# Attention and a fast three-way product on TensorE: where weights, tokens and split q and k begin in SBUF

## The chip, the core and the metric

The kernel runs on one core of one Trainium2 chip. The metric is the device time in microseconds (us) of one launch, as the median of several runs. The profile is of one execution on the same core; its span reaches from the first to the last instruction.

## What is computed

Sigmoid attention over 8 sequences, 12 heads, 448 positions, 64 values a head, and then a layer with three weight matrices and a maximum over them:

```python
scores = scale * np.matmul(q, k.transpose(0, 1, 3, 2)) - np.log(S)
attn = 1.0 / (1.0 + np.exp(-scores))
attn_out = np.matmul(attn, v).astype(np.float32)
...
x = np.ascontiguousarray(attn_out.transpose(0, 2, 1, 3)).reshape(B * S, H * D)
h = np.maximum(np.maximum(x @ w1, x @ w2), x @ w3)
return (h @ w_out).astype(np.float32)
```

There are 3584 tokens of 768 values, the four matrices are 768 x 768, and everything is float32.

## The kernel before

The program has two halves, and TensorE works in both without a pause.

**Attention** (24 steps of four heads, the loop over `fours`). Two tiles `qk` are loaded a step, each with two heads on the 128 partitions (64 partitions a head) and q and k side by side, 448 columns each. For float32 accuracy out of the faster float32r matmuls, `qk_split` (lines 287 to 297) cuts a tile into `hi` (a CAST to float32r, line 293) and `lo` (the rest, a subtraction, line 294); both are 896 columns long, q first, k behind it. `scores` (line 312) then computes k times q as three matmuls into one bank: hi with hi, lo with hi, hi with lo. The stationary operand (the weights that are loaded into the array) is a slice of 128 columns of k, the moving operand all 448 columns of q; each comes as a pair, one for the head in the lower 64 partitions and one for that in the upper 64. The last 64 rows of k go as plain float32 (`last_scores`, line 325). ACT takes the sigmoid out of PSUM (line 282), and `weigh` and `last_weigh` (lines 336 and 347) multiply it with v, as plain float32 matmuls of 64 x 64 in groups of four. DVE and ACT also decode and split the first weights meanwhile. The first step of attention splits its tiles in parts (`parts`), all other 46 tiles are split whole.

**Products** (four stages of four pairs of sequences, 16 visits, three outputs `q` a visit). Each visit uses a scheme with seven products of blocks (`PRODUCTS`) instead of eight. A product (lines 466 to 479) is nine matmuls at line 476 with three blocks of 128 rows: `wlo` with `xhi`, `whi` with `xlo`, `whi` with `xhi` for each. The stationary operand is a slice of 128 columns of a split weight tile (`whi`, `wlo`: 384 columns), the moving operand a slice of 448 columns of a split token tile (`xhi`, `xlo`: 3 x 448 columns). So there are 16 * 3 * 7 * 9 = 3024 matmuls, each with other weights than the one before. Twice in the program (`wide`) the first matmul of a product takes 478 columns instead of 448; the extra 30 columns of PSUM are not read.

**Where tiles stand.** Pools are laid out in SBUF in the order in which they are opened (lines 69 to 73): all split weights (`w`), the weight stage (`ws`), tokens (`xs`), results (`m`), and then split tokens (`xo`). The pools of attention come behind; when they are closed, the second halves of `xs` and `xo` and the small tiles of the products are laid over them. In bytes per partition, a split weight tile is 1536 long, a stage tile 1536, a token tile 5376, a result tile 1792, `qk`, `hi` and `lo` 3584.

Of the kernel before, what the change touches and what calls it, by code (L numbers as in the profile page):

```python
# [8 lines left out]
F32 = mybir.dt.float32  # L9
F32R = mybir.dt.float32r  # L10
# [3 lines left out]
ALU = mybir.AluOpType  # L14
# [3 lines left out]
P = 128  # L18
D = 64

LEAST = 1.125 * 2.0**-15

PRODUCTS = (
    ("a11", "b11", 0),
# [10 lines left out]
def attention_then_maxout(  # L35
# [9 lines left out]
    nc = tc.nc  # L45
    B, NK = qk.shape[0], qk.shape[1]
    S = qk.shape[3] // 2
# [6 lines left out]
    pin = tc.keep_in_program_order  # L54
# [11 lines left out]
    def pool(stack, name, bufs, **kw):  # L66
        return stack.enter_context(tc.tile_pool(name=name, bufs=bufs, **kw))
# [2 lines left out]
    ws_p = pool(ctx, "ws", 1)  # L70
    xs_p = [pool(ctx, "xs", 1)]
    m_p = pool(ctx, "m", 1)
    xo_p = [pool(ctx, "xo", 1)]
    ps_av = pool(ctx, "ps_av", 1, space=PSUM)

# [47 lines left out]
    def decoding(dec_p, todo, bufs, ahead, square_p):  # L123
# [11 lines left out]
        def decode(raw, out):  # L135
# [17 lines left out]
            pin(nc.vector.scalar_tensor_tensor(  # L153
                out=out, in0=square, scalar=LEAST**2, in1=bits.bitcast(F32),
                op0=ALU.is_ge, op1=ALU.mult,
# [79 lines left out]
    def attention(stack):  # L235

        qk_p = pool(stack, "qk", 4)
        hl_p = pool(stack, "hl", 2)
# [41 lines left out]
        def sigmoid(banks, **kw):  # L280
            a = a_p.tile([P, 2, S], F32, name="last" if kw else "a", **kw)
            pin(nc.scalar.activation(  # L282
                out=a, in_=banks[:, :, :S], func=AF.Sigmoid, bias=bias_s, scale=scale
            ))
            return a

        def qk_split(t, parts=(slice(0, 2 * S),)):

            hi = hl_p.tile([P, 2 * S], F32R, name="hi")
            lo = hl_p.tile([P, 2 * S], F32R, name="lo")  # L290
            for cols in parts:
                high = hi[:, cols]
                pin(nc.vector.tensor_copy(out=high, in_=t[:, cols]))
                pin(nc.vector.tensor_tensor(
                    out=lo[:, cols], in0=t[:, cols], in1=high.bitcast(F32), op=ALU.subtract
                ))
            return (hi, hi), (hi, lo), (lo, hi)

        def accumulators():
            return ps_av.tile([P, 2, 512], F32, name="ps_av")  # L300
# [1 line left out]
        def halves(ps):  # L302
            return [ps[:, e] for e in range(2)]

        def scores(terms, c, banks=None):
            if banks is None:
                banks = ps_s.tile([P, 2, 512], F32, name="ps_s")
            bank = halves(banks)
            for n, (kt, qt) in enumerate(terms):
                for e in range(2):  # L310
                    r = slice(e * D, (e + 1) * D)
                    pin(nc.tensor.matmul(  # L312
                        bank[e][:, :S], kt[r, S + c * P : S + (c + 1) * P], qt[r, :S],
                        start=n == 0, stop=n == len(terms) - 1,
                    ))
            return sigmoid(banks)
# [36 lines left out]
        loads = {}  # L353
# [26 lines left out]
        for n in range(12):  # L380
            e = n % 2
            idle = nc.const_aps.tensor(0.0, [D, P], F32, start_partition=e * D)
            pin(nc.tensor.matmul(ps[:, e, :P], idle, idle, start=True, stop=True))  # L383
        xs, lasts = {}, {}
        terms = [[(loads[0][0],) * 2]]
        end = len(fours) - 1
        for n in range(len(fours)):
            ts = loads.pop(n)
# [12 lines left out]
            if n == 0:  # L401
                chunks = [slice(S + c * P, S + (c + 1) * P) for c in range(1, C)]
                split = qk_split(ts[0], [slice(0, S)] + chunks)
                terms = (terms[0],) + (split,) * (C - 1)
                cut = S + P
                terms += (qk_split(ts[1], (slice(0, cut), slice(cut, S + C * P))),)
            else:
                terms = (terms[0],) * C + (terms[1],)
            first = [scores(terms[c], c) for c in range(C)]
            if n == 0:  # L410
                held = accumulators()
                last_scores(ts, held)
                load(n + 2)
                vts[n + 1] = load_v(*fours[n + 1])
            ahead = loads.get(n + 1)
            after = [qk_split(ahead[0]) if ahead else None]
            second = []
            for c in range(C):
                second.append(
                    scores(terms[C], c, accumulators() if n and c == 0 else None)  # L420
                )
                if n == c == 0:
                    lasts[n] = sigmoid(held, bufs=2)
            after.append(qk_split(ahead[1]) if ahead else None)
            terms = after
# [30 lines left out]
    with ExitStack() as stack:  # L456
        xs, finish = attention(stack)
# [202 lines left out]
```

## Time and profile before

| | us |
|---|---|
| median of 3 runs | 864.51 (864.01 to 864.61) |
| span of the profiled execution | 861.9 |
| TensorE busy in it | 857.6 |
| DVE busy | 619.9 |
| ACT busy | 413.3 |
| POOL busy | 173.5 |

The profiled execution has no other time of its own than its span; the median of the runs is 2.6 us above it, for what lies before the first and behind the last instruction. Busy shares overlap, as the engines work at the same time. A matmul is shown from its start to the (modelled) end of its results, and the next one starts before that end, so the distance of starts tells the rate, not the length.

### The profile page before, as it was taken

How to read it: one execution, taken by the hardware profiler on the slowest of the kernel's cores; microseconds unless marked ns; L12 is line 12 of the kernel's file. 1: busy time of each engine (PE TensorE's matmuls, PEld its weight loads, DVE VectorE, ACT ScalarE, POOL GpSimd, SP SyncE). 2: the span in 40 equal slices, each digit the busy share in tenths (PEclk: the TensorE clock that was granted, in tenths of full speed). 3: DMA queues.
4: the chain of work that ended last, by engine and by line, in shares of the span. 5: the costliest groups of instructions: out<-in, count | busy, mean ns of one | idle time of the engine just before them, and what ended most of it. 6: DMA issues, size and time to landing. Idle time of an engine off the chain costs nothing.

```text
span 861.9 us, 14260 instructions
## 1 busy us (share of the span) xinstructions
PE 857.6 (99%) x5446; PEld 706.5 (82%) x5446; DVE 619.9 (72%) x885; ACT 413.3 (48%) x545; POOL 173.5 (20%) x148
## 2 busy tenths in 40 slices
PE   9999999999999999999999999999999999999998
PEld 5555555555579999999999999999999999999997
DVE  5677668877795775787887698778778887736542
ACT  6888888888862340423434252234325252423310
POOL 0010020202115337121000021200002544560600
PEclk9999999999999999999999999999999999999999
DMA  8657776786684537326563823465472516153412
GB/s 293 209 209 242 246 253 231 257 295 220 214 288 175 184 147 250 125 75 205 207 248 113 324 80 97 161 254 198 161 290 99 186 43 238 69 202 123 154 65 86
DMA packets 74628, 161.96 MB, mean 188 GB/s; under 512 B 6976, under 2 KB 54080, under 8 KB 74560
## 3 DMA queue, kind: packets, MB, share of 16 engines
q1 hardware_dynamic: 74416, 160.94, 53.0%
q8 instruction: 43, 0.70, 0.3%
q14 instruction: 25, 0.20, 0.1%
q10 hardware_dynamic: 144, 0.11, 0.0%
HBM read 109.90 MB, written 51.12 MB: 187 GB/s over the span
## 4 chain that ended last, share of the span: by engine, by line
PE 99%; DVE 0%; DVEq 0%; issue 0%
PE ps_y L476 71%; PE ps_s L312 9%; PE ps_s L336 7%; PE ps_av L336 6%; PE ps_s L347 2%; PE ps_s L325 2%; PE ps_av L312 2%; PE ps_s L383 0%; PE ps_av L325 0%; PE ps_av L347 0%; DVE m L548 0%; DVEq L656 0%
## 5 line engine op out<-in xcount | busy, mean ns | idle before, releaser
L476 PE MATMUL ps_y<-xhi_t,whi_s 128*128 128x448 f32 x432 | 157.9, 365 | 0.0
L476 PE MATMUL ps_y<-xhi_t,wlo_s 128*128 128x448 f32 (+1 forms) x432 | 157.8, 365 | 0.0
L476 PE MATMUL ps_y<-xlo_t,whi_s 128*128 128x448 f32 x432 | 157.8, 365 | 0.0
L282 ACT ACTIVATE a<-ps_s,bias_s 128x896 f32<-128x896 f32 x121 | 114.5, 1016 | 10.2 <-PE ps_s L312 10.2
L476 PE MATMUL ps_y<-xhi_b,wlo_a 128*128 128x448 f32 x288 | 105.3, 366 | 0.0
L476 PE MATMUL ps_y<-xlo_b,whi_a 128*128 128x448 f32 x288 | 105.2, 365 | 0.0
L476 PE MATMUL ps_y<-xhi_b,whi_a 128*128 128x448 f32 x288 | 105.2, 365 | 0.0
L583 ACT COPY p<-ps_y 128x448 f32<-128x448 f32 x48 | 25.5, 531 | 157.6 <-PE ps_y L476 157.6
L108 POOL TENSOR_TENSOR ws_s<-ws_a,ws_a 128x384 f32<-128x384 f32 x12 | 14.2, 1180 | 417.9 <-DMA ws_a<-w_dram 312.8
L476 PEld LDWEIGHTS ps_y<-xhi_t,whi_s 128*128 128x128 f32 x432 | 81.2, 188 | 6.4
L476 PEld LDWEIGHTS ps_y<-xlo_t,whi_s 128*128 128x128 f32 x432 | 81.2, 188 | 6.4
L476 PEld LDWEIGHTS ps_y<-xhi_t,wlo_s 128*128 128x128 f32 x432 | 81.2, 188 | 6.3
L557 DVE TENSOR_TENSOR m<-ps_y,u 128x448 f32<-128x448 f32 x71 | 43.9, 621 | 53.3 <-PE ps_y L476 53.3
L544 ACT COPY m<-ps_y 128x448 f32<-128x448 f32 x24 | 12.8, 533 | 124.8 <-PE ps_y L476 112.6
L586 DVE TENSOR_TENSOR u<-ps_y,p 128x448 f32<-128x448 f32 x48 | 29.9, 623 | 53.9 <-PE ps_y L476 50.3
L196 POOL TENSOR_TENSOR xs_t<-xs_b,xs_t 128x448 f32<-128x448 f32 x48 | 59.8, 1272 | 38.9 <-PE ps_s L325 26.8
L231 DVE TENSOR_TENSOR xlo_t<-xs_t,xhi_t 128x1344 fp32r<-128x1344 f32 x42 | 66.7, 1589 | 0.0
L231 DVE TENSOR_TENSOR xlo_b<-xs_b,xhi_b 128x1344 fp32r<-128x1344 f32 x42 | 66.5, 1584 | 0.0
L142 ACT ACTIVATE c<-wraw 128x384 f32<-128x384 f32 x48 | 27.4, 570 | 75.5 <-DVE m L563 44.0
L336 PE MATMUL ps_av<-a,v 64*64 64x448 f32 x576 | 62.6, 536 | 0.0
L227 ACT CAST xhi_t<-xs_t 128x1344 fp32r<-128x1344 f32 x41 | 54.2, 1323 | 12.4 <-PE ps_y L476 8.8
L336 PE MATMUL ps_s<-a,v 64*64 64x448 f32 x576 | 59.7, 545 | 0.0
(89 smaller groups left out, 1769.0 us busy)
## 6 DMA issues: line engine op xcount, KB each, us to landing
qk<-qk SPq DMA_DIRECT2D x47, 448.0 KB, 4.6
xs_b<-x_dram SPq DMA_DIRECT2D x30, 672.0 KB, 6.9
wraw<-w SPq DMA_DIRECT2D x36, 384.0 KB, 4.8
xs_t<-t_dram SPq DMA_DIRECT2D x18, 672.0 KB, 8.0
v<-v SPq DMA_DIRECT2D x24, 448.0 KB, 5.5
h_dram<-m SPq DMA_DIRECT2D x48, 224.0 KB, 1.9
xs_b<-h_dram SPq DMA_DIRECT2D x16, 672.0 KB, 6.2
x_dram<-m SPq DMA_DIRECT2D x47, 224.0 KB, 3.0
```

Source lines behind the costliest of these rows:

```text
L142: pin(nc.scalar.activation(out=square, in_=high.bitcast(F32), func=AF.Square))
L196: pin(nc.gpsimd.tensor_tensor(out=r[name][:, k], in0=r[in0][:, k], in1=r[in1][:, k], op=ALU.subtract))
L227: pin(copy(out=hi, in_=r[name]))
L231: pin(nc.vector.tensor_tensor(out=lo, in0=x, in1=hi.bitcast(F32), op=ALU.subtract))
L282: pin(nc.scalar.activation(out=a, in_=banks[:, :, :S], func=AF.Sigmoid, bias=bias_s, scale=scale))
L312: pin(nc.tensor.matmul(bank[e][:, :S], kt[r, S + c * P : S + (c + 1) * P], qt[r, :S], start=n == 0, stop=n == len(terms) - 1,))
L325: pin(nc.tensor.matmul(ps[g * D : (g + 1) * D, e, :S], t[r, S + C * P :], t[r, :S], start=True, stop=True,))
L336: pin(nc.tensor.matmul(ps[e * D : (e + 1) * D, :S], vt[rows, (g * C + c) * 2 + e], chunks[c][rows, e], start=c == 0 and not (ahead and r = ...
L476: pin(nc.tensor.matmul(ps[:, :cols], wt[:, k * P : (k + 1) * P], moving, start=first and n == 0, stop=n == len(terms) - 1, skip_group_chec ...
L557: pin(nc.vector.tensor_tensor(out=m[name], in0=y, in1=add, op=ALU.add))
L583: pin(nc.scalar.copy(out=p1, in_=ps[0][:, :S]))
L586: pin(nc.vector.tensor_tensor(out=u2, in0=ps[1][:, :S], in1=p1, op=ALU.add))
```

## The change

An unused tile of 16 words (64 bytes) is opened between the results and the split tokens. All tiles behind it move by 64 bytes, the split tokens among them; weights stay. In attention, `hi` and `lo` become 1024 columns long, and where a tile is split whole, k begins at column 496 (`KEYS`) instead of 448, so 48 words between q and k are not used. Both split instructions then write two pieces of 448 columns, with a gap, instead of one of 896. `scores` gets q and k as two views. Where a tile is split in parts (the first step), k stays at column 448. The plain float32 matmuls read `qk`, `a`, `last` and `v`, which only move as a whole.

```diff
+SHIFT = 16
+
+KEYS = 496
...
     m_p = pool(ctx, "m", 1)
+
+    pool(ctx, "shift", 1).tile([P, SHIFT], F32, name="shift")
     xo_p = [pool(ctx, "xo", 1)]
...
-        def qk_split(t, parts=(slice(0, 2 * S),)):
-
-            hi = hl_p.tile([P, 2 * S], F32R, name="hi")
-            lo = hl_p.tile([P, 2 * S], F32R, name="lo")
-            for cols in parts:
-                high = hi[:, cols]
-                pin(nc.vector.tensor_copy(out=high, in_=t[:, cols]))
+        def qk_split(t, parts=None):
+
+            hi, lo = [hl_p.tile([P, 1024], F32R, name=name) for name in ("hi", "lo")]
+            if parts is None:
+                at, src = KEYS, t[:].rearrange("p (e c) -> p e c", e=2)
+                out = [x[:, : 2 * KEYS].rearrange("p (e c) -> p e c", e=2)[:, :, :S] for x in (hi, lo)]
+                views = [(src, *out)]
+            else:
+                at, views = S, [[x[:, cols] for x in (t, hi, lo)] for cols in parts]
+            for src, high, low in views:
+                pin(nc.vector.tensor_copy(out=high, in_=src))
                 pin(nc.vector.tensor_tensor(
-                    out=lo[:, cols], in0=t[:, cols], in1=high.bitcast(F32), op=ALU.subtract
+                    out=low, in0=src, in1=high.bitcast(F32), op=ALU.subtract
                 ))
-            return (hi, hi), (hi, lo), (lo, hi)
+            (hk, hq), (lk, lq) = [(x[:, at : at + S], x[:, :S]) for x in (hi, lo)]
+            return (hk, hq), (hk, lq), (lk, hq)
...
-                        bank[e][:, :S], kt[r, S + c * P : S + (c + 1) * P], qt[r, :S],
+                        bank[e][:, :S], kt[r, c * P : (c + 1) * P], qt[r],
...
-        terms = [[(loads[0][0],) * 2]]
+        terms = [[(loads[0][0][:, S:], loads[0][0][:, :S])]]
```

No instruction is added, removed or moved on any engine. The one thing that reads otherwise in the order of the instructions is the shape of the 46 whole splits on DVE, here of the second step of attention:

```order
18 L293 CAST hi<-qk 128x896
19 L294 TENSOR_TENSOR lo<-qk,hi 128x896
20 L293 CAST hi<-qk 128x896
21 L294 TENSOR_TENSOR lo<-qk,hi 128x896
22 L144 TENSOR_SCALAR wb<-wraw 128x384
```

and the same place with the change:

```order
18 L304 CAST hi<-qk 128x2x448
19 L305 TENSOR_TENSOR lo<-qk,hi 128x2x448
20 L304 CAST hi<-qk 128x2x448
21 L305 TENSOR_TENSOR lo<-qk,hi 128x2x448
22 L151 TENSOR_SCALAR wb<-wraw 128x384
```

The rows stand at the same places; only the shapes of the four splits differ.

## Rows read from the trace of the kernel before

**Rows 1.** The page: busy time, granted clock in 40 slices, chain that ended last.

```profile
PE 857.6 (99%) x5446; PEld 706.5 (82%) x5446; DVE 619.9 (72%) x885; ACT 413.3 (48%) x545; POOL 173.5 (20%) x148
...
PEclk9999999999999999999999999999999999999999
...
PE 99%; DVE 0%; DVEq 0%; issue 0%
PE ps_y L476 71%; PE ps_s L312 9%; PE ps_s L336 7%; PE ps_av L336 6%; PE ps_s L347 2%; PE ps_s L325 2%; PE ps_av L312 2%; PE ps_s L383 0%; PE ps_av L325 0%; PE ps_av L347 0%; DVE m L548 0%; DVEq L656 0%
```

**Rows 2.** Windows of 100 us in the products, all engines: work and instructions of each.

```profile
core 0: us, PE busy (x) PEld busy (x) DVE busy (x) ACT busy (x) POOL busy (x), PEclk, DMA share, GB/s
250.00:350.00 100.00, 100.00 (x495) 92.76 (x494) 66.87 (x82) 26.46 (x30) 49.85 (x40) 1.00 0.55 201
...
550.00:650.00 100.00, 100.00 (x495) 92.75 (x494) 74.79 (x111) 33.90 (x46) 6.32 (x7) 1.00 0.64 231
650.00:750.00 100.00, 100.00 (x496) 92.72 (x495) 82.99 (x104) 43.87 (x58) 45.64 (x34) 1.00 0.35 122
750.00:850.00 100.00, 100.00 (x495) 92.74 (x494) 47.98 (x55) 26.63 (x30) 26.78 (x24) 1.00 0.36 129
```

**Rows 3.** Timeline of TensorE: the first product and the beginning of the second.

```profile
start us, us, engine line op out<-in xcount [idle before <-releaser]
...
245.18 0.48 PE L476 MATMUL ps_y<-xhi_b,wlo_a 128*128 128x448 f32 x1
245.49 0.36 PE L476 MATMUL ps_y<-xlo_b,whi_a 128*128 128x448 f32 x1
...
247.14 0.38 PE L476 MATMUL ps_y<-xhi_t,wlo_s 128*128 128x478 f32 x1
247.36 0.36 PE L476 MATMUL ps_y<-xlo_t,whi_s 128*128 128x448 f32 x1
```

**Rows 4.** Timeline of TensorE: 32 starts near 300 us (first, last), and the program's last matmul.

```profile
299.64 0.37 PE L476 MATMUL ps_y<-xlo_t,whi_s 128*128 128x448 f32 x1
...
305.92 0.36 PE L476 MATMUL ps_y<-xhi_t,whi_a 128*128 128x448 f32 x1
...
858.00 0.37 PE L476 MATMUL ps_y<-xhi_b,whi_s 128*128 128x448 f32 x1
```

**Rows 5.** Timeline of TensorE in attention: 17 pairs of line 312 (first, last).

```profile
66.11 0.36 PE L312 MATMUL ps_s<-lo,hi 64*128 64x448 f32 x2
...
69.35 0.36 PE L312 MATMUL ps_s<-hi,lo 64*128 64x448 f32 x2
```

**Rows 6.** Timeline of TensorE in attention: plain float32 matmuls, merged where they repeat.

```profile
60.81 1.31 PE L336 MATMUL ps_s<-a,v 64*64 64x448 f32 x12
61.94 0.54 PE L347 MATMUL ps_s<-last,v 64*64 64x448 f32 x2
```

**Rows 7.** Lines 476 and 312: duration ns min/median/max, first and last start.

```profile
L476 PE MATMUL ps_y<-xlo_t,whi_s x432: 360/365/370, 247.4 to 852.3; 128*128 128x448 f32 x144
...
L476 PE MATMUL ps_y<-xhi_t,whi_s x432: 361/365/370, 247.6 to 852.5; 128*128 128x448 f32 x144
...
L312 PE MATMUL ps_s<-lo,hi x240: 354/362/468, 5.2 to 239.3; 64*128 64x448 f32 x120
...
L312 PE MATMUL ps_s<-hi,lo x240: 356/362/367, 5.4 to 239.5; 64*128 64x448 f32 x120
```

**Rows 8.** Groups by form: the splits on DVE, and weight loads that waited for one.

```profile
line engine op names shapes xcount | busy us, mean ns | idle before us <-releasers
...
L294 DVE TENSOR_TENSOR lo<-qk,hi 128x896 fp32r<-128x896 f32 x46 | 51.1, 1110 | 1.6
...
L293 DVE CAST hi<-qk 128x896 fp32r<-128x896 f32 x46 | 30.1, 654 | 10.6 <-PE ps_s L312 8.8 <-DMA qk<-qk 1.0
...
L312 PEld LDWEIGHTS ps_s<-hi 64*128 64x128 f32 x240 | 22.5, 184 | 19.0 <-issue 16.2 <-DVE hi L293 0.7 <-ACT a L282 0.7
...
L294 DVE TENSOR_TENSOR lo<-qk,hi 128x448 fp32r<-128x448 f32 x1 | 0.6, 626 | 0.0
...
L293 DVE CAST hi<-qk 128x448 fp32r<-128x448 f32 x1 | 0.4, 394 | 2.8 <-DMA qk<-qk 2.8
```

**Rows 9.** Window of 20 us in attention, all engines.

```profile
60.00:80.00 20.00, 20.00 (x204) 11.30 (x200) 16.03 (x29) 16.70 (x23) 0.00 (x0) 1.00 0.70 240
```

## The prediction, made before the changed kernel ran

> **What bounds the kernel now.** I read the shares of the page first, then the rate of TensorE stage by stage, then single starts. [Rows 1] say that TensorE is busy for 857.6 of 861.9 us, at the full granted clock of 2.4 GHz (9 in every slice; 1.00 in the stretches of [rows 2]), and that the chain that ended last is TensorE for 99%, 71% of it line 476, the nine matmuls of each product of the second half. No other engine and no transfer shows in that chain. So nothing that makes another engine faster or slower counts here as long as it stays covered; what counts is how far apart matmuls start.
>
> "Busy" doesn't tell that distance, because matmuls overlap: one is shown 365 ns long [rows 7], while the next starts long before it ends. The starts do. The first of the 3024 product matmuls starts at 245.18 us [rows 3], the last at 858.00 us [rows 4]: 612.82 us / 3023 = **202.7 ns** from start to start. A stretch in the middle gives the same: 31 steps in 6.28 us, 202.6 ns [rows 4]. In the attention half the matmuls of split q and k run in pairs (one for each half of the partitions), and 16 steps from pair to pair take 3.24 us, 202.5 ns [rows 5].
>
> How much of this is streaming? At 2.4 GHz 448 columns take 186.7 ns if one goes in per cycle. The trace has a row near that: the plain float32 matmuls of 64 partitions come in fours, and three fours take 1.13 us (60.81 to 61.94) [rows 6], 376.7 ns each, which is twice 188.3 ns. I take 188.3 ns as the distance of an unhindered stream of 448 columns; that such a four is two clean passes is an inference. Then each step of 202.7 ns holds 14.4 ns in which TensorE neither streams nor waits for another engine.
>
> Where do these 14.4 ns come from? Three things in the rows narrow it down. First, they don't depend on the rest of the core: over four stretches of 100 us DVE goes from 48.0 to 83.0 us of work, ACT from 26.5 to 43.9, POOL from 6.3 to 49.9, transfers from 122 to 231 GB/s, and TensorE starts 495 or 496 matmuls in each [rows 2]. So it is between TensorE's own two readings of SBUF, the moving tokens and the weights of the next matmul, which start nearly together. Second, they aren't constant: the same instruction on the same shape is shown 360 to 370 ns long at line 476, and 354 to 367 ns (leaving out first ones) at line 312 [rows 7]. Third, and most telling, the same work has been run at two distances in this very trace: in the first product the eight steps from 245.49 to 247.14 take 1.65 us, 206.3 ns each; then one matmul of 478 columns stands between, and from there on it is 202.7 ns [rows 3, 4]. Thirty extra columns, once, changed the rate of all that follows. A fixed cost per matmul can't do that; two readers that fall into step with each other, and lose time when they want the same part of SBUF, can. Their step then depends on when each starts and on where each starts.
>
> **Where they start, and what the change does to that.** From the tile sizes: every tile before is a multiple of 256 bytes long as far as TensorE reads it (a weight slice is 512 bytes, a token slice 1792, k starts 1792 bytes behind q), so moving and stationary operand of every matmul begin at the same remainder by 256 bytes. After it, tokens begin 64 bytes further on than weights by that remainder; and k begins 496 * 4 = 1984 = 7 * 256 + 192 bytes behind q, which again puts the weights (k) 64 bytes behind the moving operand (q). So all 3024 product matmuls and the pairs of the 46 large splits get one new relation, the same in both halves. Of 429 pairs of line 312 with split operands (858 matmuls: 240 * 3 + 46 * 3), the 15 of the first step of attention, split in parts, keep the old layout: 414 change.
>
> **The edits, costed.**
>
> - *Tokens 64 bytes further on.* No row shows this relation, so the step is bounded from both sides. Below: the unhindered 188.3 ns [rows 6], 14.4 ns less. Above: the 206.3 ns of the first product [rows 3], 3.6 ns more. Between these I take the row that stands nearest to "same matmul, fewer lost cycles": the shortest matmuls of line 476 are 360 or 361 ns against a median of 365 [rows 7], 4.5 ns shorter. If all were as the shortest are now, the step is 198.2 ns: 3024 * 4.5 ns = 13.6 us less. (At the ends: 3024 * 14.4 = 43.5 us less, 3024 * 3.6 = 10.9 us more.)
> - *48 words between q and k.* Same relation, same price: 414 * 4.5 ns = 1.9 us less (ends: 6.0 less, 1.5 more).
> - *The splits in two pieces.* The 46 large CASTs and subtractions now step over a gap in the tile that they write; count and elements are the same. Bounds: nothing, or the price of two separate pieces of 448: 2 * 394 - 654 = 134 ns and 2 * 626 - 1110 = 142 ns [rows 8], 0.28 us a split. I take nothing on the path: DVE has 16.0 us of work in a 20 us stretch of attention [rows 9], with four splits in it, so even 4 * 0.28 = 1.1 us fits into the 4 us left. TensorE waited for such a CAST once, for 0.7 us [rows 8]; without the cover, at most 46 * 0.28 = 13 us would appear.
> - *Longer tiles.* The split tiles are 4096 instead of 3584 bytes long, and what is placed behind them moves. No instruction changes its place on any engine; two get one more wait at the seam between the halves: an ACT CAST of tokens on a transfer, and a transfer of coded weights on TensorE. Both wait for attention work that is over by then; I take zero. If they were late, TensorE would show a hole just behind 245 us; the nearest price is the step of 314 ns that is there now (245.18 to 245.49 [rows 3]).
>
> Sum: 13.6 + 1.9 = 15.5 us off the span of 861.9, 846.4 us. The median of the runs, 864.5, stands 2.6 us above that span; I keep this difference: **849.0 us**.
>
> The Trainium skill speaks against the change. "TensorE: Matmul & The Clock Gate", Part 2, says of the two read ports that loading the next weights takes no SBUF bandwidth from the running matmul, and "SBUF — State Buffer", Who interferes with whom, lets only the pair of ports shared by VectorE and GpSimd contend; by these, addresses don't matter and the sum is zero. Yet the first page's Back-to-back issue gap, N / 2.4 + 2.5, gives an estimate of 189.2 ns for 448 columns, 13.5 ns under the 202.7 ns of this trace, and the two distances of [rows 3, 4] don't fit a stream that nothing hinders. I follow the trace; the pages' case is the second rival.
>
> **The rivals.**
>
> - *The collisions go altogether.* With the new relation the two readers never meet again. The step falls to between 188.3 and 195 ns. For it: the clean fours of [rows 6] show that a stream beside weight loads can be clean. Against it: those loads are of 64 columns, half as long, and both readers walk over many times 256 bytes in one matmul, so a shifted start may only move the meeting. Time: at 188.3 ns 3438 * 14.4 = 49.5 us less, 815 us; at 195 ns (7.7 less) 838 us.
> - *Nothing moves.* Either the lost time doesn't depend on where operands start, only on when (30 columns changed the when), or the shift doesn't reach the tiles as I worked it out. Time: 864.5 us. For it: 202.7 in products and 202.5 in attention, though pairs of 64 partitions are a different pattern.
> - *It falls into the slow step.* The 478-column matmuls of the old kernel stay where they are; with the new relation the readers may lock into a state like that of the first product, and a widening by 30 columns may lead into it instead of out. Place: every product after the widened matmul. Price: 3.6 * 3438 = 12.4 us more, **877 us**; it decides from the point where the step is over 203.2 ns (0.5 * 3438 = 1.7 us). For it: this state exists here [rows 3]. Against it: it ended after nine matmuls and the later step held for 610 us.
>
> **How the numbers follow.** A measurement of this kernel can tell about 0.2%, 1.7 us, from no change. Forecast (step 195 to 201 ns): 0.38. All collisions gone: 0.21. A smaller gain, step 201 to 202.2: 0.03. Nothing: 0.17. Slower: 0.21. So faster 0.62, same 0.17, slower 0.21. The range must leave out 0.2: half of the clean case (below 824 us, a step of about 191 ns) and half of the slower one (above 872 us, about 204.9 ns): 824 to 872 us. It holds both signs; the forecast's own range is 838 to 859 (steps of 195 and 201 ns).
>
> **What would show it.** Right: starts of the product matmuls stand 198 ns apart from the second product to the end, pairs in attention about as far, with engines' work unchanged, and the spread of matmul lengths narrower. The clock stays at full. Two-piece splits keep near 650 and 1110 ns. Wrong: a step unchanged with all else; a step under 195 ns or over 203; a gain in one half only, which would speak for two different causes; or a hole at the seam behind the last attention matmul.

## The result and the profile after

The changed kernel takes 857.0 us (median of 4 runs, 856.5 to 857.1) against 864.3 us before (863.4 to 864.6): ratio 0.9916, interval 0.9902 to 0.9930. It is 7.3 us faster, where I forecast 15.5. The sign and the place were right; the price was about double what came. Of 43 runs of the kernel before on record, 39 took 863.4 to 865.0 us and four 867.0 to 871.8; all 18 runs of this kernel and of the three below that also hold the tokens 64 bytes further on (tokens_only, no_wide, best64) took 856.0 to 857.3. A run's time is 1.8 us above its own span in every run that lists both, so 0.8 of the 2.6 us between median and span before is a difference between two executions; the forecast of a difference does not hang on it.

The page after, busy time and chain; it answers to [rows 1] (all line numbers below are those of the changed kernel, where 476 became 488, 312 became 324 and 336 became 348):

```profile
span 855.3 us, 14262 instructions
...
PE 851.0 (99%) x5446; PEld 704.7 (82%) x5446; DVE 618.3 (72%) x885; ACT 412.8 (48%) x545; POOL 174.7 (20%) x148
...
PEclk9999999999999999999999999999999999999999
...
PE 99%; DVE 0%; DVEq 0%; issue 0%
```

Nothing in it says what happened: the same chain, the same shares, the clock full. The windows do, beside [rows 2]:

```profile
core 0: us, PE busy (x) PEld busy (x) DVE busy (x) ACT busy (x) POOL busy (x), PEclk, DMA share, GB/s
250.00:350.00 100.00, 100.00 (x502) 93.74 (x501) 67.63 (x82) 27.77 (x31) 49.81 (x40) 1.00 0.56 201
550.00:650.00 100.00, 100.00 (x502) 93.75 (x501) 74.72 (x109) 34.80 (x48) 8.34 (x8) 1.00 0.62 229
650.00:750.00 100.00, 100.00 (x499) 92.71 (x498) 81.70 (x103) 43.13 (x57) 43.91 (x32) 1.00 0.38 126
```

The count of matmuls in 100 us went from 495 to 502, by the same 7 whether POOL works 50 us or 8. In the third stretch it went only from 496 to 499: new waits, listed below, fall there, and seven longer steps cost 0.66 us, the time of three matmuls. The single starts of line 488 give the step; first the beginning of the product stage, then 34 starts near 300 us and the last matmul of the program (all from the timeline of TensorE):

```profile
245.85 0.47 PE L488 MATMUL ps_y<-xhi_b,wlo_a 128*128 128x448 f32 x1
246.16 0.36 PE L488 MATMUL ps_y<-xlo_b,whi_a 128*128 128x448 f32 x1
...
247.77 0.37 PE L488 MATMUL ps_y<-xhi_t,wlo_s 128*128 128x478 f32 x1
247.98 0.36 PE L488 MATMUL ps_y<-xlo_t,whi_s 128*128 128x448 f32 x1
...
299.38 0.36 PE L488 MATMUL ps_y<-xhi_t,wlo_s 128*128 128x448 f32 x1
...
305.98 0.36 PE L488 MATMUL ps_y<-xhi_t,wlo_a 128*128 128x448 f32 x1
...
851.37 0.36 PE L488 MATMUL ps_y<-xhi_b,whi_s 128*128 128x448 f32 x1
```

33 steps in 6.60 us are **200.0 ns** each, against 202.6 in [rows 4]. The first product steps at 1.61 us / 8 = 201 ns already, against 206 in [rows 3]. The whole stage, from its first to its last start, takes 605.52 us instead of 612.82: 7.3 us less, the whole of the gain. 3023 * 2.7 = 8.2 us would be the step alone; most of the rest went to new waits. TensorE now runs ahead of DVE now and then (waits of its weight loads at line 488):

```profile
PEld ps_y L488 <- DVE wb L155: 0.7, 1, 0.7
PEld ps_y L488 <- DVE xlo_b L238: 0.6, 2, 0.3
PEld ps_y L488 <- DVE c L574: 0.5, 2, 0.3
...
PEld ps_y L488 <- DVE xlo_t L238: 0.2, 1, 0.2
```

Only the first of these was there before; the others are 1.3 us on waiting loads, and the steps there are longer by about 0.7 us in all.

Attention gained nothing. In the same block as [rows 5], pairs follow each other a little faster (16 steps in 3.22 us instead of 3.24), but the block as a whole, from its first pair to the first matmul with v, is as long as ever:

```profile
66.35 0.47 PE L324 MATMUL ps_s<-hi 64*128 64x448 f32 x2
66.66 0.36 PE L324 MATMUL ps_s<-lo,hi 64*128 64x448 f32 x2
...
69.88 0.37 PE L324 MATMUL ps_s<-hi,lo 64*128 64x448 f32 x2
70.19 1.34 PE L348 MATMUL ps_s<-a,v 64*64 64x448 f32 x9
```

66.35 to 70.19 is 3.84 us; before, it was 65.81 to 69.64, 3.83 us. (The product stage even begins 0.67 us later than before, which is why the span fell by 6.6 us and the stage by 7.3. 0.58 us of it is there when the scores of the second step of attention begin, at 16.27 us instead of 15.69. They begin at 16.13 us in old_no_wide below, where q and k stand to each other as before, so this start does not hang on the change.) The splits in two pieces cost nothing at all, as taken (the profile merges their shape to 896 again; 655 and 1110 ns against 654 and 1110 in [rows 8]):

```profile
L305 DVE TENSOR_TENSOR lo<-qk,hi 128x896 fp32r<-128x896 f32 x46 | 51.1, 1110 | 1.6
L304 DVE CAST hi<-qk 128x896 fp32r<-128x896 f32 x46 | 30.1, 655 | 9.8 <-PE ps_s L324 8.7 <-DMA qk<-qk 0.5
```

### The profile page after: what moved, and what is told of

It is laid out like the page before. It is cut to its first block, busy times and chain, and to the rows that moved or that the text cites. A ratio compares the mean times of both kernels' runs of the same rounds, so it can differ in the third digit from the quotient of the medians.

```text
span 855.3 us, 14262 instructions
## 1 busy us (share of the span) xinstructions
PE 851.0 (99%) x5446; PEld 704.7 (82%) x5446; DVE 618.3 (72%) x885; ACT 412.8 (48%) x545; POOL 174.7 (20%) x148
## 4 chain that ended last, share of the span: by engine, by line
PE 99%; DVE 0%; DVEq 0%; issue 0%
PE ps_y L488 71%; PE ps_s L324 9%; PE ps_s L348 7%; PE ps_av L348 6%; PE ps_s L359 2%; PE ps_s L337 2%; PE ps_av L324 2%; PE ps_s L395 0%; PE ps_av L337 0%; PE ps_av L359 0%; DVE m L560 0%; DVEq L668 0%
## 5 line engine op out<-in xcount | busy, mean ns | idle before, releaser
L115 POOL TENSOR_TENSOR ws_s<-ws_a,ws_a 128x384 f32<-128x384 f32 x12 | 12.3, 1028 | 413.7 <-DMA ws_a<-w_dram 307.9
```

## The experiments

Theory: the step of a matmul depends on how the moving and the stationary operand stand to each other by the remainder by 256 bytes, and the tokens carry the gain. Rivals: it is the tokens' own place; it is the splits in attention; the widened matmuls hold it. All edits are against the changed kernel.

**The two halves of the change apart, the place alone, and without widening.**

tokens_only, `-KEYS = 496` `+KEYS = 448`:

> The unused 64 bytes before the split tokens alone; q and k lie side by side as before. If the distance of product matmuls is set by where tokens begin against weights, products step at 200.0 ns as with the whole change and nearly all of the gain stays: 857 to 858 us, and pairs of attention step at 202.5 ns. If the gain came from both halves alike (14% of the relevant matmuls are in attention), a seventh of it goes: 858 us. If the gain comes from the gap between q and k, 864 us.

keys_only, without the unused tile:

```diff
-    pool(ctx, "shift", 1).tile([P, SHIFT], F32, name="shift")
```

> The 48 words between q and k alone. By the theory of start addresses, pairs of attention step at 200 ns and products at 202.7 ns: 414 * 2.5 ns = 1 us less at most, 863 to 864.5 us; less is left where attention then waits for the sigmoids of ACT. If pairs don't count, 864.3 us with a step of 202.5 ns.

all_moved, the unused tile ahead of the weights, and k at 448:

```diff
+    pool(ctx, "front", 1).tile([P, 16], F32, name="front")
     w_p = pool(ctx, "w", 1)
...
-    pool(ctx, "shift", 1).tile([P, SHIFT], F32, name="shift")
```

> 64 unused bytes ahead of the weights, none between weights and tokens, q and k side by side: every tile lies 64 bytes further on, so each tile stands where the change puts it (split tokens begin at multiples of 256 bytes), but weights and tokens begin at the same remainder by 256 bytes again. If the relation of the two operands counts: product step 202.7 ns, 864.3 us. If the place of the tokens itself counts (multiples of 256 bytes): 200.0 ns and 857 us.

no_wide:

```diff
-    wide = (0, 0, 1), (done - len(pairs) - 1, 1, 4)
+    wide = ()
```

> The whole change, and no matmul of 478 columns any more (both places take 448). If the new relation has one step whatever came before, 200.0 ns from the first products on and 857 us. If the widened matmul still leads out of a slower state, the step stays at what the first product shows or more (206 ns would be 875 us).

Measured, with before at 864.2 us beside them: tokens_only 856.6 us (ratio 0.9911, 0.9896 to 0.9925), keys_only 864.2 (0.9991, 0.9973 to 1.0009), all_moved 864.4 (1.0009, 0.9991 to 1.0026), no_wide 856.8 (0.9911, 0.9896 to 0.9926). Windows of tokens_only, then of all_moved:

```profile
300.00:400.00 100.00, 100.00 (x502) 93.71 (x501) 77.83 (x105) 32.04 (x44) 33.97 (x28) 1.00 0.41 148
```

```profile
300.00:400.00 100.00, 100.00 (x495) 92.68 (x495) 77.24 (x105) 31.55 (x43) 34.90 (x28) 1.00 0.40 143
```

The relation carries it, not the place of the tokens by itself: all_moved puts the split tokens where the change puts them, with the weights moved as far, and has 495 matmuls in 100 us, tokens_only 502. The whole gain is the tokens'. With the new relation the widened matmuls are not needed.

keys_only explains why attention gave nothing. Its block, timeline of TensorE (line numbers one lower):

```profile
66.59 0.47 PE L323 MATMUL ps_s<-hi 64*128 64x448 f32 x2
...
70.10 0.37 PE L323 MATMUL ps_s<-hi,lo 64*128 64x448 f32 x2
70.43 0.98 PE L347 MATMUL ps_s<-a,v 64*64 64x448 f32 x8
```

66.59 to 70.43 is 3.84 us again. The last step of the block, from the last pair to the first matmul with v, grew from 0.29 (69.35 to 69.64 before) to 0.33 us. That matmul needs sigmoids, and the weight loads of these matmuls wait for ACT a little longer, 7.8 us in 24 blocks instead of 7.2. What pairs save, the wait for the last sigmoid takes back. It is so in the mean of the 23 blocks of 18 pairs: from the first pair to the last 3.524 us instead of 3.549, from there to the first matmul with v 0.316 instead of 0.287. (In the keys_only trace, then in that of before, groups by form:)

```profile
L347 PEld LDWEIGHTS ps_s<-a,v 64*64 64x64 f32 x576 | 19.7, 132 | 29.2 <-issue 21.4 <-ACT a L288 7.8
```

```profile
L336 PEld LDWEIGHTS ps_s<-a,v 64*64 64x64 f32 x576 | 19.6, 133 | 28.6 <-issue 21.4 <-ACT a L282 7.2
```

**Other distances**, each with the same one between the operands of attention; and the kernel before without widening, old_no_wide (the changed kernel with the unused tile out, `KEYS = 448`, `wide = ()`; its split tiles keep the length of the change). The diff is that of off256; `SHIFT` and `KEYS` are 32 and 480 for off128, 48 and 464 for off192, 8 and 504 for off32, 24 and 488 for off96, 40 and 472 for off160, 56 and 456 for off224.

```diff
-SHIFT = 16
+SHIFT = 64
...
-KEYS = 496
+KEYS = 512
```

> 256 unused bytes between weights and tokens and 64 words (256 bytes) between q and k: the operands begin at the same remainder by 256 bytes again, but not by 512. If the remainder by 256 bytes is what counts, product step 202.7 ns, pairs 202.3 to 203.3 ns, about 864 us. If any distance from the old place helps, or the period is longer, another step; 200.0 ns would be 857 us.

> 128 unused bytes, and 32 words between q and k (weights begin 128 bytes behind the moving operand by the remainder by 256). If every relation but the equal one is alike: 200.0 ns, 857 us. If the step follows the remainder in steps of 64 bytes, another value between 188 and 207 ns; I can't say which. If the period is 128 bytes instead of 256: 202.7 ns.

> 192 unused bytes, and 16 words between q and k (weights begin 64 bytes ahead of the moving operand instead of behind it). If only being apart by 64 bytes counts: 200.0 ns, 857 us. If the order counts (who meets whom first), another step than 200.0 ns.

> The kernel before without its two matmuls of 478 columns (448 there too). If the widened matmul led the old relation out of a slower step, as I read from the first product, 206 ns stays to the end: 3.6 * 3024 = 11 us more, 875 us. If the first product was slow only because it was the first, 202.7 ns and 864 us.

> 32 unused bytes, k 32 bytes behind q's remainder less (56 words of gap). So far the product step is 202.67 ns at 0 and 256 bytes, 200.00 at 64, 204.00 at 128, 202.22 at 192. If 64 bytes are the unit (the readers meet in blocks of 64 bytes), 32 lies in the same block as 0 or gives something mixed: 200 to 203 ns, 857 to 865 us. If the step changes smoothly: about 201 ns, 860 us. A step far under 198 ns would mean that a place without collisions lies between the ones tried: under 851 us.

> 96 unused bytes, 40 words between q and k. Smooth: about 202 ns, 862 us. In blocks of 64 bytes: 200.0 ns as at 64. Under 198 ns: a place without collisions, which I think unlikely now that four places all cost 11 to 16 ns over a clean pass.

> 160 unused bytes, 24 words between q and k. Smooth: about 203 ns, 866 us. In blocks of 64 bytes: 204.0 ns as at 128, 868 us.

> 224 unused bytes, 8 words between q and k. Smooth: about 202.4 ns, 863 us. In blocks of 64 bytes: 202.2 ns as at 192, 863 us.

Measured, one run each (before beside them: 864.1 us for the first four, 865.0 us for the last four). The mean step is (last start - first start) / 3023 of the product matmuls, from the timelines:

| bytes between | first start | last start | mean step, ns | run, us |
|---|---|---|---|---|
| 0 (before) | 245.18 | 858.00 | 202.7 | 864.3 |
| 0, no widening | 245.61 | 870.46 | 206.7 | 876.2 |
| 32 | 246.48 | 871.32 | 206.7 | 877.1 |
| 64 (the change) | 245.85 | 851.37 | 200.3 | 857.0 |
| 96 | 246.66 | 867.51 | 205.4 | 873.2 |
| 128 | 246.55 | 863.36 | 204.0 | 869.1 |
| 160 | 245.47 | 850.59 | 200.2 | 856.3 |
| 192 | 245.57 | 857.02 | 202.3 | 862.7 |
| 224 | 246.85 | 865.01 | 204.5 | 870.7 |
| 256 | 245.63 | 858.45 | 202.7 | 864.2 |

The step is the same at 256 as at 0, and not at 64 or 128, so, as far as these few places show, it repeats after 256 bytes and no sooner. In between it goes neither smoothly nor in blocks of 64 bytes: my expectations for 32, 96, 160 and 224 bytes all failed. No place gives less than 200.0 ns, and four of the seven new distances are slower than before. Each place but 64 bytes has one run here, so a row is the step that this run settled on; best160 below shows a second one at 160 bytes.

The widened matmuls are in all of these kernels but old_no_wide, twice. At 0 and 256 bytes the first of them changes the rate, from 206.0 ns in the eight steps of the first product to 202.7; at the other distances these eight steps lie within 1.1 ns of the later rate, so there the widening does not set it. The second, some 440 us later, leaves the rate as it is in all these traces. So old_no_wide shows that thirty columns at the start decide 4 ns a matmul for 600 us: the same program without them stays at 206.7 ns (window of old_no_wide).

```profile
300.00:400.00 100.00, 100.00 (x486) 90.83 (x485) 75.56 (x101) 31.93 (x44) 35.43 (x29) 1.00 0.39 140
```

**What holds 200.0 ns?** Two explanations were tried: the columns and a fixed cost, or a step rounded up to a whole unit. Beside them ran the version that keeps only what matters.

cols440 (first edit; it leaves tokens out, so its results are incomplete) and cols464 (second edit), both with `KEYS = 448` and `wide = ()`:

```diff
-            moving, cols = xt[:, k], S
-            if wide and n == 0:
-                cols = S + 30
-                moving = xt[:].rearrange("p a s -> p (a s)")[:, :cols]
+            cols = S if n == 0 else S - 8
+            moving = xt[:, k, :cols]
```

```diff
+            cols = S + 16 if k < HALF - 1 else S
+            moving = xt[:].rearrange("p a s -> p (a s)")[:, k * S : k * S + cols]
```

> 64 bytes before the tokens, q and k side by side, no matmul of 478 columns, and eight of the nine matmuls of each product take 440 columns instead of 448: the last 8 tokens of each block are left out of all but the first of its nine matmuls. The steps measured so far (200.0, 202.2, 202.67, 204.0, 204.4, 205.33, 206.67 ns) are all simple fractions of 13.33 ns, the time of 32 columns at 2.4 GHz, and the best is 15 of them, where 448 columns are 14. If a step in the even state is rounded up to whole units of 13.33 ns, 440 columns (13.75 units) fit into 14: 186.7 ns for eight of nine, 30 to 36 us less than 857, 821 to 827 us if DVE and ACT keep up. If a matmul costs its columns and a fixed 13.3 ns, 3.3 ns less for each of 2688: 848 us.

> 64 bytes before the tokens, q and k side by side, no matmul of 478 columns, and six of the nine matmuls of each product take 464 columns instead of 448 (the 16 extra columns of PSUM are not read; nothing is left out). Rounded up to whole units of 13.33 ns: 464 columns are 14.5 units, the step stays 200.0 ns, 856 to 857 us. Columns and a fixed 13.3 ns: 6.7 ns more for each of 2016, 870 us.

best64 (`KEYS = 448`, `wide = ()`) and best160 (the same with `SHIFT = 40`):

> Only what the runs show to matter: 64 bytes before the tokens, q and k side by side, no matmul of 478 columns. Product step 200.0 ns; against the whole change it saves two times 10 to 14 ns and the slightly longer step to the sigmoids: 856.5 us, not to be told from the change, 0.9% under before.

> As best64 with 160 bytes instead of 64, the other place with a step of 200.0 ns, there with every single step equal. 856 to 856.5 us; if even steps leave fewer waits for DVE than 201, 201, 198, some 0.3 us under best64.

Measured, with before at 864.0 us beside them: cols440 856.0 us, cols464 881.1 (one run each), best64 856.4 (0.9901, 0.9883 to 0.9919), best160 859.1 (0.9953, 0.9922 to 0.9983). Both explanations of 200 ns fell. Windows of cols440, then of cols464:

```profile
300.00:400.00 100.00, 100.00 (x501) 93.93 (x501) 74.93 (x104) 32.05 (x44) 34.52 (x28) 1.00 0.42 149
```

```profile
300.00:400.00 100.00, 100.00 (x483) 90.29 (x482) 74.08 (x99) 32.04 (x44) 36.24 (x29) 1.00 0.40 141
```

With 8 columns less the rate is what it was (501 in 100 us), neither 3.3 nor 13.3 ns better; with 16 more in six of nine it falls to 483, a mean step of 208 ns, worse than the 204.4 ns that columns alone would give and far from the unchanged 200.0 of the rounding.

best160 ran from 855.9 to 867.4 us, and its profiled run (867.4) shows what happened in that one; windows, then the timeline where they change:

```profile
405.00:505.00 100.00, 100.00 (x501) 93.84 (x501) 78.28 (x116) 37.85 (x51) 4.36 (x4) 1.00 0.58 214
525.00:625.00 100.00, 100.00 (x485) 90.50 (x484) 78.38 (x125) 37.12 (x59) 8.59 (x8) 1.00 0.51 182
```

```profile
508.23 0.36 PE L488 MATMUL ps_y<-xhi_t,whi_a 128*128 128x448 f32 x1
508.43 0.42 PE L488 MATMUL ps_y<-xhi_b,wlo_s 128*128 128x448 f32 x1
508.68 0.36 PE L488 MATMUL ps_y<-xlo_b,whi_s 128*128 128x448 f32 x1
...
509.29 0.37 PE L488 MATMUL ps_y<-xlo_b,whi_s 128*128 128x448 f32 x1
509.50 0.37 PE L488 MATMUL ps_y<-xhi_b,whi_s 128*128 128x448 f32 x1
```

TensorE steps at 200.0 ns until 508.43 us, waits for DVE once (0.25 us to the next start instead of 0.20; 0.2 us put down to line 574), and from there to the end steps at 206.7 ns: 485 matmuls in 100 us instead of 501. At 160 bytes there are two steps that hold by themselves, and in this trace the change from one to the other comes at a short wait. A wait need not bring it: in off160 five steps of 223 to 308 ns, at three places, were followed by 200.0 ns again. The other eleven runs of best160 have no trace: six took 855.9 to 857.2 us, three 861.0 to 862.1, two 866.9 and 867.4. An estimate fits them: in best64 TensorE waits around the steps 1314, 2134 and 2320 of 3023, and going from 200.0 to 206.7 ns there would cost some 11.4, 5.9 and 4.7 us; no trace shows that it happened there. At 64 bytes the waits listed above left no such trace: after each the step is 200.0 ns again.

**The round of the weight loads.** Loads are 188 ns long, with some 12 ns to the next; that makes 200. half_loads and half_loads440 are best64 with loads of 64 instead of 128 weight columns in seven of the nine matmuls of a product (they leave out half of the output rows there); half_loads440 also takes 440 columns, as cols440 does:

```diff
+            rows = P if n in (0, len(terms) - 1) else D
...
-                ps[:, :cols], wt[:, k * P : (k + 1) * P], moving,
+                ps[:rows, :cols], wt[:, k * P : k * P + rows], moving,
```

> best64, but seven of the nine matmuls of each product load 64 weight columns instead of 128 and write 64 rows of PSUM (the other 64 output rows get only the first and the last term). If 200.0 ns is the round of the weight loads (188 ns of load and 12 ns until the next), seven of nine steps fall towards the columns' 188 to 195 ns, 133 ns being the length of a load of 64 columns: mean step 190 to 196 ns, 825 to 844 us. If something else holds the step at 200.0 ns: 856 us.

> half_loads with 440 moving columns in all but the first matmul of a product (the last 8 tokens of a block and half of the output rows are left out of these). If with short loads the moving columns are the bound, 8 columns are worth 3.3 ns now, where they were worth nothing with full loads: 7 to 10 us less than half_loads. If another round holds both, the two are alike.

Measured: 864.0 and 857.3 us (before beside them 863.4). Windows of half_loads, then of half_loads440:

```profile
300.00:400.00 100.00, 100.00 (x496) 72.15 (x495) 77.57 (x105) 31.51 (x43) 34.91 (x28) 1.00 0.40 143
```

```profile
300.00:400.00 100.00, 100.00 (x502) 72.94 (x501) 76.20 (x105) 32.03 (x44) 34.91 (x28) 1.00 0.41 147
```

The loads fell from 94% of the time to 72%, and the mean step did not get under 200 ns: half_loads is slower than best64 (202.6 ns), half_loads440 returns to 200.4. So the loads' own length is not what keeps the step from falling. What holds 200.0 ns is open. "Trainium Kernel Development and Optimization" of the Trainium skill, Performance Expectations, calls the busy share of weight loads a good measure of the distance to the limit; here the same rate, 502 matmuls in 100 us, came with 94% and, where most loads were shorter, with 73%.

## Why the prediction was right or wrong

- **What bounds the kernel** was right: the distance of starts, not the busy share; and the lost time is TensorE's own. Away from the new waits the rate changed by the same 7 matmuls in 100 us whatever the other engines did.
- **Where the lost time comes from** was right in what could be tested: the relation of the two operands' starts (tokens_only against all_moved) and the history (old_no_wide, best160). That they collide in the same part of SBUF was argued, and no run shows the part.
- **The step that failed** is the price of "Tokens 64 bytes further on": 4.5 ns a matmul, 13.6 us. It measured 2.7 ns (202.7 to 200.0), 8.2 us, less the new waits 7.3 us. The 4.5 ns came from the spread of shown lengths [rows 7], 360 or 361 against 365. That spread is no reserve. After the change it did get narrower, as I had said, but from above: the shortest lengths are still 360 ns, the median is 362 or 363, and starts still alternate, with steps of 201, 201 and 198 ns in turn. The shortest of a wavering series was taken for a state in which all could be. The 857.0 us still lies inside the range that I gave to the forecast (838 to 859 us), near its slow end. Line 488 after the change:

```profile
L488 PE MATMUL ps_y<-xlo_t,whi_s x432: 360/362/363, 248.0 to 845.8; 128*128 128x448 f32 x144
L488 PE MATMUL ps_y<-xhi_t,whi_s x432: 360/363/363, 248.2 to 846.0; 128*128 128x448 f32 x144
```
- **The floor of 188.3 ns** [rows 6], which carried the rival with 0.21 of the chance, was reached by none of these matmuls. Nine distances, fewer columns and shorter loads gave 200.0 ns at best. I should not have read a floor for float32r from plain float32 in fours of 64 x 64: loads as short as theirs (half_loads) did not bring it. Nor are those half as long as the others, as I wrote: they take 133 ns, the others 188.
- **48 words between q and k**: 1.9 us forecast, nothing came. The pairs did get faster, but I had not asked who waits behind them. The first matmul with v waits for the last sigmoid, and took back what the pairs gave (3.83 us a block before, 3.84 after).
- **Splits in two pieces, longer tiles**: nothing, as taken. The hole at the seam is the 0.31 us it was (245.85 to 246.16).
- **The rival that nothing moves** fell: the address relation alone moves the step, between 200.0 ns at 64 bytes and 206.7 at 32 in programs that otherwise differ only in the gap between q and k. "SBUF — State Buffer" of the Trainium skill, Who interferes with whom, says that only the port pair shared by VectorE and GpSimd contends. By that rule the step would have stayed at 202.7 ns, so here the measurement decides; whether TensorE's two reads contend, or something else depends on where they start, no run shows. **The slow rival** was a real state, only not at 64 bytes: at 32, 96, 128 and 224 bytes the change would have been a loss of 5 to 12 us (one run each).

## What to carry to other kernels

Where TensorE is busy all the time, take the distance of matmul starts over hundreds of them, and if it is over the columns' time, try where the two operands begin relative to each other by the remainder by 256 bytes: an unused tile is all it takes, but each distance has to be measured, because the curve is neither smooth nor monotone and half of it is worse. Choose a distance that also holds after waits (64 bytes here), not only one that is fast in a single run (160 bytes), and do it only where nothing but TensorE is waited for: in attention, with ACT one sigmoid behind, it brought nothing. Of this change, the 64 bytes alone (best64, 856.4 us) do as much as all of it.

## What the runs showed of the hardware that I had not expected

- A stretch of equal matmuls settles on a step and keeps it for hundreds of microseconds: 206.7 or 202.7 ns with equal remainders, 206.7 or 200.0 ns at 160 bytes. Thirty columns once (old_no_wide) moved it from one to another, and in one trace (best160) it changed at a wait of 0.2 us; longer waits left it where it was in off160 and at 64 bytes.
- Taking 8 of 448 columns off changed nothing at 200.0 ns; adding 16 to six of nine cost more than their streaming (208 ns on average where columns alone would give 204.4).
- Halving most weight loads did not shorten the step, and made it longer at 448 columns (202.6 ns). Which resource keeps 200 ns is not known from these runs.
